# Windowed attention and two feed-forward layers on one core: blocks of 32 queries by 64 keys in place of 64 by 96, and an order of all steps read from a stored list

## The chip, the cores and the metric

The kernel runs on one core of a Trainium2 chip. The metric is the device time of one launch in microseconds (us), the median of several runs. Beside it there is one profiled execution, whose trace gives the start and end of every instruction and every transfer.

## What is computed

The reference, cut to what matters:

```python
def _attn_ref(q, k, v):                       # 4 x 8 x 576 x 64 (batch, heads, positions, width)
    scores = np.matmul(q, k.transpose(0, 1, 3, 2)) / np.sqrt(D)
    rel = pos[:, None] - pos[None, :]
    mask_plain = (rel >= 0) & (rel < 32)                        # heads 0 to 3
    mask_dil = (rel >= 0) & (rel < 128) & (rel % 4 == 0)        # heads 4 to 7
    scores = np.where(masks[None], scores, -1e9)
    attn = np.exp(scores - np.max(scores, axis=-1, keepdims=True))
    attn = attn / (np.sum(attn, axis=-1, keepdims=True) + 1e-09)
    return np.matmul(attn, v)

def _moe_ref(x, w_in, w_out, g_ln):           # 2304 x 512 -> 1024 -> 512
    h = x @ w_in
    sm = softmax(h)                           # max, exp, sum + 1e-9, over the 1024
    solu = h * sm
    ln = (solu - mean(solu)) / np.sqrt(var(solu) + 1e-06) * g_ln
    return ln @ w_out

def _moe2_ref(x, w_in, w_out):                # 2304 x 512 -> 2048 -> 512
    h = x @ w_in
    return (h * (1.0 / (1.0 + np.exp(-1.702 * h)))) @ w_out

def reference(...):
    x = _attn_ref(q, k, v) laid out as (batch * positions) x (heads * width)
    return _moe2_ref(_moe_ref(x, ...), ...)
```

A query looks at itself and 31 keys ahead of it; in the dilated heads these are every fourth position. If the positions of a dilated head are reordered into four streams, its window is 32 neighbours as well.

## The kernel before, in words

**Attention.** A batch has five *units*. Units 0 to 3 hold two heads each and the first 512 queries of both; the fifth, a half unit, holds the last 64 queries of all eight heads. That makes 16 full units and 4 half units. A full unit is cut into eight windows of `QW` = 64 queries by `KW` = 96 keys (the 64 and the 32 ahead of them). Its steps are small functions:

- `att_s` (TensorE): 16 score multiplications (line 235), one for each head and window, each with 64 rows (the width) by 64 queries as the weights and 96 keys as the moving columns. Two heads lie on two halves of the rows, two windows on two halves of the output partitions. In batches 0 and 1 (`PE_MASK`) two multiplications with an identity first put the mask into the result (line 231); in batches 2 and 3 VectorE adds it (`att_mask`).
- `att_max`, `att_sub`, `att_exp`, `att_sum` (line 301), `att_norm` (line 308) on VectorE, ScalarE and GpSimd: the softmax, over 768 columns of a full unit and 384 of a half one.
- `att_t` (TensorE): eight transposes of 128 x 96 (line 316), four into one bank of the PSUM, called once for each head; `att_p` copies each bank out (line 322).
- `att_x` (TensorE): 16 multiplications of the transposed probabilities with v (line 332): 96 rows, 64 columns of v as the weights, 64 queries moving. `att_y` copies the result into `x` (lines 350 to 358), in the order that the positions need.

`stir` (line 217) issues up to 16 filler multiplications ahead of some of these steps, as many as the planner's gap suggests.

**First feed-forward layer.** Weights arrive as raw 64-bit words, are converted to fp32 (lines 377 to 393) and split into a high and a low part (`split_hi`; `split_lo`, lines 441 and 445; `wo_l` is the low part of `w_out`). Each product takes three multiplications (high by high, low by high, high by low). Per tile of 128 tokens there are two halves of `h` (line 472, twelve records of 512 columns each), then the maximum (line 480), exp (486), the product with the softmax (494), the layer norm, transposes `lt` (523), and their split `lnh` (531) and `lnl` (534). For each 256 tokens the second product `y` follows (line 545). The first `y` needs the whole converted `w_out`.

**Second feed-forward layer.** Its weights are split while the first layer runs ("parked", lines 377 to 393 and 584 to 614) and written back to memory. The products are made in seven instead of eight block products (`h_prod` line 666, `o_plain` 748, `o_prod` 779), with sums on VectorE around them. At the end `ob` is summed (line 801) and stored.

**Order.** Every step is put into a `Plan` with a rank, an engine (or several), a cost, the steps it comes after, and slots that it takes and gives back (PSUM banks, buffers). `Plan.order` then plays the engines forward with these costs: whenever an engine is free, it takes the ready step of lowest rank. `emit` writes the steps in that order and ties each engine's instructions to it, so each queue is fixed before the launch. The ranks are worked out by the code from the lists `LOADS`, `HEAD`, `PARK` and others; the loads on SP's queue are steps too.

Of the kernel before, what the change touches and what calls it, by code (L numbers as in the profile page):

```python
# [24 lines left out]
QW = 64  # L25
KW = QW + 32
NW = S // QW
UB = 5
WM = NW - 1
# [32 lines left out]
class Plan:  # L62
# [5 lines left out]
    def add(self, rank, eng, cost, fn, after=(), take=(), give=(), lag=0.12, also=(), port=False):  # L68
        can = {eng: (cost, fn, port or eng == "POOL")}
        can.update({e: (c, f, port or e == "POOL") for e, c, f in also})  # L70
        self.works.append(Work(len(self.works), rank, can, after, take, give, lag))
        return self.works[-1]

    def order(self):
# [6 lines left out]
        while any(left.values()):  # L81
# [4 lines left out]
            for eng, works in left.items():  # L86
                while free[eng] <= t:
# [3 lines left out]
                    for w in works:  # L91
                        if any(t < r < t + w.can[eng][0] - 0.2 and w.key[0] - k >= 5 for k, r in soon):
# [41 lines left out]
def attention_moe_kernel(ctx, tc, qk, qk_last, v, v_last, masks, w_in, w_out, g_ln, w2_in, w2_out, out):  # L134
# [23 lines left out]
    for g in range(3):  # L158
# [20 lines left out]
    nq, nk, nv = WM * QW, WM * QW + 32, 2 * WM * D  # L179
    flat = [y1[g].rearrange("p k n -> p (k n)") for g in range(3)]  # L180
    lent = {2: (flat[0][:, 0:nq], flat[0][:, nq:nq + nk], flat[1][0:KW, 0:nv]),
            3: (flat[0][:, nq + nk:2 * nq + nk], flat[1][:, nv:nv + nk], flat[2][0:KW, 0:nv])}
# [14 lines left out]
    def load_v(idx):  # L197
        v_ = lent[idx][2] if idx in lent else ap.tile([KW, nv], F32, tag="v", bufs=VB, name=f"v{idx}")
        nc.sync.dma_start(v_, v[idx])
        vW[idx] = v_.rearrange("p (h w d) -> p h w d", h=2, w=WM)  # L200

    def load_last(b):

        t = ap.tile([P, 4, QW + KW], F32, tag="qkl", bufs=LB, name=f"qkl{b}")
        nc.sync.dma_start(t.rearrange("p i c -> p (i c)"), qk_last[b])
        vt = ap.tile([KW, 4, 2, D], F32, tag="vl", bufs=LB, name=f"vl{b}")
        nc.sync.dma_start(vt.rearrange("p i h d -> p (i h d)"), v_last[b])
# [14 lines left out]
    def att_s(n):  # L222
# [3 lines left out]
        if u < 4:  # L226
# [5 lines left out]
            for wp in range(4):  # L232
                for h, par in ((0, 0), (1, 1), (0, 1), (1, 0)):
                    rows, c = slice(64 * h, 64 * h + 64), QW * (2 * wp + par)
                    nc.tensor.matmul(ps[64 * par:64 * par + 64, h, wp * KW:wp * KW + KW], q_[rows, c:c + QW],  # L235
                                     k_[rows, c:c + KW], start=not masked, stop=not masked or wp == 3)
            sps[n] = ps[:, :, 0:4 * KW]
        else:
# [4 lines left out]
            for i in range(4):  # L243
                for h in range(2):
                    rows = slice(64 * h, 64 * h + 64)
                    nc.tensor.matmul(ps[rows, i * KW:i * KW + KW], last_w[b][0][rows, i, 0:QW],
                                     last_w[b][0][rows, i, QW:], start=not masked, stop=not masked or i == 3)
# [1146 lines left out]
```

## Time and profile before

| what | value |
|---|---|
| runs | 677.69, 676.4, 676.84 us; median 676.84 |
| span of the profiled execution (its time, first to last instruction) | 675.9 us |
| TensorE (PE) busy | 653.8 us, 97%, 4921 instructions |
| weight loads on TensorE (PEld) | 617.3 us, 91% |
| VectorE (DVE) | 524.2 us, 78% |
| ScalarE (ACT) | 386.6 us, 57% |
| GpSimd (POOL) | 126.3 us, 19% |
| DMA | 155.55 MB, mean 230 GB/s |

The span is 0.9 us under the median of the runs; no time of its own is given for the profiled execution beyond it. Busy time of an engine counts overlapping instructions once. PE's matmuls are pipelined: a row's duration is that of one instruction from start to end, while the next one starts before it has ended, so the cost of a stream is read from the distance of the starts. A group such as "x32" in the timeline gives the start of the first and the time to the end of the last. One `nc.tensor.matmul` with fp32 operands appears as two records (16 score multiplications are 32 records), one with fp32r or bf16 operands as one.

### The profile page before, as it was taken

The numbers are of one execution on the slowest core, as the hardware profiler recorded it, in microseconds if no ns is written. First come the engines' busy times: TensorE is split into PE (matmuls) and PEld (weight loads), VectorE is DVE, ScalarE is ACT, GpSimd is POOL, SyncE is SP. The second block draws the span as 40 slices with busy tenths as digits, with TensorE's granted clock in tenths as the row PEclk, the third lists the DMA queues.
The fourth block names the chain that finished last, engine by engine and source line by source line (L and its number), as shares of the span: only waits on it lengthen the run. The fifth ranks groups of instructions, "written<-read, shape, count | busy, mean of one in ns | idle before, by whom it ended". The sixth has DMA issues, their size and how long they took to land.

```text
span 675.9 us, 12935 instructions
## 1 busy us (share of the span) xinstructions
PE 653.8 (97%) x4921; PEld 617.3 (91%) x4921; DVE 524.2 (78%) x950; ACT 386.6 (57%) x789; POOL 126.3 (19%) x146
## 2 busy tenths in 40 slices
PE   6798999999999999999999999999999999999997
PEld 4676898888888898999999999999999999999997
DVE  3999977684776798789867899378699948778794
ACT  4898967485656776775335765242365534334552
POOL 0305373353532443433000000000000000000000
PEclk9889999999999999999999999999999999999999
DMA  8899126534221566986768886767699866679952
GB/s 294 287 309 284 49 88 238 186 134 153 73 100 63 197 243 228 324 304 216 270 225 290 310 292 241 280 242 285 232 312 329 297 227 206 238 247 319 328 184 84
DMA packets 58254, 155.55 MB, mean 230 GB/s; under 512 B 6608, under 2 KB 21968, under 8 KB 58192
## 3 DMA queue, kind: packets, MB, share of 16 engines
q1 hardware_dynamic: 58192, 154.72, 67.2%
q8 instruction: 39, 0.64, 0.4%
q14 instruction: 23, 0.19, 0.1%
HBM read 118.53 MB, written 36.18 MB: 229 GB/s over the span
## 4 chain that ended last, share of the span: by engine, by line
PE 74%; DVE 11%; DMA 8%; issue 2%; ACT 2%; POOL 1%; SPq 0%; ACTq 0%; DVEq 0%; POOLq 0%
PE hz L666 14%; PE h L472 12%; PE hx L666 11%; PE oz L779 10%; PE y L545 9%; PE ox L779 7%; PE ob L748 2%; PE ptp L316 2%; PE oa L748 2%; PE lt L523 2%; PE xt L332 1%; PE s L235 1%; DMA y<-in_w_in_dram 1%; DMA raw_('o', 3, 0)_4712<-in_w_out_dram 1%; DMA raw_('o', 1, 1)_3957<-in_w_out_dram 1%
## 5 line engine op out<-in xcount | busy, mean ns | idle before, releaser
L666 PE MATMUL hz<-yc,ws 128*128 128x384 f32 x576 | 107.5, 334 | 1.3 <-DVE u L678 1.3
L718 ACT CAST gs<-g 128x384 fp32r<-128x384 f32 x144 | 72.9, 514 | 59.1 <-PE oz L779 25.4
L666 PEld LDWEIGHTS hz<-yc,ws 128*128 128x128 f32 x576 | 100.5, 188 | 1.6 <-DVE u L678 1.6
L721 DVE TENSOR_TENSOR gs<-g,gs 128x384 fp32r<-128x384 f32 x144 | 78.2, 554 | 15.9 <-ACT gs L718 15.1
L666 PE MATMUL hx<-yc,ws 128*128 128x384 f32 x432 | 83.5, 335 | 2.0 <-DVE p L674 0.8
L545 PE MATMUL y<-lnh,wo_h 128*128 128x256 f32 x288 | 83.0, 288 | 0.0
L545 PE MATMUL y<-lnh,wo_l 128*128 128x256 f32 x288 | 81.5, 283 | 0.0
L545 PE MATMUL y<-lnl,wo_h 128*128 128x256 f32 x288 | 81.4, 283 | 0.0
L666 PEld LDWEIGHTS hx<-yc,ws 128*128 128x128 f32 x432 | 75.3, 188 | 3.2 <-DVE p L674 1.2
L472 PE MATMUL h<-wi_h,xh 128*128 128x512 f32 x144 | 58.9, 409 | 0.0
L472 PE MATMUL h<-wi_l,xh 128*128 128x512 f32 x144 | 56.4, 392 | 0.0
L472 PE MATMUL h<-wi_h,xl 128*128 128x512 f32 x144 | 56.4, 391 | 0.0
L545 PEld LDWEIGHTS y<-lnh,wo_h 128*128 128x128 f32 x288 | 55.1, 191 | 1.0
L545 PEld LDWEIGHTS y<-lnl,wo_h 128*128 128x128 f32 x288 | 55.1, 191 | 0.3
L545 PEld LDWEIGHTS y<-lnh,wo_l 128*128 128x128 f32 x288 | 55.1, 191 | 0.0
L695 ACT ACTIVATE sg<-g 128x768 f32<-128x768 f32 (+1 forms) x48 | 33.0, 687 | 32.4 <-DVE g L686 27.1
L695 ACT ACTIVATE sg<-hx 128x384 f32<-128x384 f32 x24 | 11.8, 492 | 50.8 <-PE hx L666 45.8
L779 PE MATMUL oz<-gs,wo 128*128 128x384 f32 x192 | 36.8, 335 | 0.0
L779 PE MATMUL ox<-gs,wo 128*128 128x384 f32 x192 | 36.7, 334 | 0.0
L308 POOL TENSOR_TENSOR t<-t,sx 128x768 f32<-128x768 f32 (+1 forms) x17 | 23.4, 1375 | 65.7 <-DVE sx L303 41.4
L779 PEld LDWEIGHTS oz<-gs,wo 128*128 128x128 f32 x192 | 33.5, 188 | 0.2 <-DVE gs L721 0.2
L779 PE MATMUL oz<-gs,w 128*128 128x384 f32 x192 | 33.6, 334 | 0.0
(391 smaller groups left out, 1412.6 us busy)
## 6 DMA issues: line engine op xcount, KB each, us to landing
ws<-wdq SPq DMA_DIRECT2D x48, 512.0 KB, 5.0
wo<-wdo SPq DMA_DIRECT2D x37, 512.0 KB, 5.3
ws<-wdq SPq DMA_DIRECT2D x48, 384.0 KB, 5.0
w<-wdo SPq DMA_DIRECT2D x48, 256.0 KB, 4.6
qk<-in_qk_dram SPq DMA_DIRECT2D x14, 528.0 KB, 5.2
v<-in_v_dram SPq DMA_DIRECT2D x14, 384.0 KB, 4.2
y<-in_w_in_dram SPq DMA_DIRECT2D x9, 512.0 KB, 4.9
wdq<-y SPq DMA_DIRECT2D x9, 512.0 KB, 3.0
```

The lines of the kernel that those rows point to most:

```text
L235: nc.tensor.matmul(ps[64 * par:64 * par + 64, h, wp * KW:wp * KW + KW], q_[rows, c:c + QW], k_[rows, c:c + KW], start=not masked, stop=not ...
L308: eng.tensor_tensor(t, t, wide(sms.pop(n), t.shape[1]), ALU.mult)
L316: nc.tensor.transpose(ps[:, j * P:j * P + P], t[:, 4 * h + j, :], ident)
L472: nc.tensor.matmul(hps[i][:, half, :], x[:, kt, :], w[:, kt, fs], start=(kt == 0 and j == 0), stop=(kt == KT - 1 and j == 2))
L523: nc.tensor.transpose(ps[:, j, :], es[i][:, f * P:f * P + P], ident)
L545: nc.tensor.matmul(yps[g, dm][:, 0:n], w[:, f, ds_], x[:, f, 0:n], start=(f == 0 and j == 0), stop=(f == NF1 - 1 and j == 2))
L666: nc.tensor.matmul(ps[:, 0:TB2], quad_weights(q, m, kk, a), yc2[m][:, x, kk, :], start=(m < 4 and kk == 0 and i == 0), stop=(kk == 1 and i ...
L695: nc.scalar.activation(sg, src, AF.Sigmoid, scale=1.702)
L718: nc.scalar.copy(gsp[jj, m][:, 0], o_block(jj, half, b))
L721: nc.vector.tensor_tensor(gsp[jj, m][:, 1], o_block(jj, half, b), f32(gsp[jj, m][:, 0]), ALU.subtract)
L748: nc.tensor.matmul(ps, w[:, (2 * k + a) * P:(2 * k + a + 1) * P], gsp[jj, 2 * half + b][:, x], start=first and i == 0, stop=last and i == 2)
L779: nc.tensor.matmul(ps, w, gsp[jj, m][:, x], start=m < 4 and first and i == 0, stop=last and i == 2, skip_group_check=True)
```

## The change

Blocks become `QB` = 32 queries by `KW` = 64 keys. A full unit has 16 blocks for each head. Its parts:

- **Scores.** 32 multiplications of 64 rows by 32 queries, 64 moving columns, on eight tiles of the array (two heads on the rows, four blocks on the output partitions), in a rotation written out. The mask multiplications have 256 columns for 384. A unit's softmax works on 512 columns for 768, a half unit's on 256 for 384.
- **Transposes.** Two neighbouring blocks of 64 keys are transposed together, 128 x 128, so a full unit has four transposes for eight, in one bank, and one copy of 128 x 512 for two of 96 x 512.
- **v** is laid out for 128 partitions: blocks of even and odd pairs on the two halves, each with its 64 keys, so a unit's v is 512 KB for 384. It is done on the host, as before.
- **Product with v.** 32 multiplications of 64 rows, 64 columns of v as the weights, 32 moving queries, into two banks; for the plain heads the output is written in runs of 8. `att_y` copies each bank by itself.
- **Order.** `add` takes the rank from the list `ORDER`, one number for each step, instead of the computed one; a few steps get one more predecessor, the costs of the attention steps are lower, a slot "mx" is new. The rule of `order` that lets a waiting urgent step hold back others no longer asks for a distance of five ranks.

```diff
-QW = 64
-KW = QW + 32
+QB = 32
+KW = 2 * QB
...
     def add(self, rank, eng, cost, fn, after=(), take=(), give=(), lag=0.12, also=(), port=False):
         can = {eng: (cost, fn, port or eng == "POOL")}
         can.update({e: (c, f, port or e == "POOL") for e, c, f in also})
+        rank = ORDER[len(self.works)] if ORDER else rank
...
-                        if any(t < r < t + w.can[eng][0] - 0.2 and w.key[0] - k >= 5 for k, r in soon):
+                        if any(t < r < t + w.can[eng][0] - 0.2 and w.key[0] > k for k, r in soon):
...
-        v_ = lent[idx][2] if idx in lent else ap.tile([KW, nv], F32, tag="v", bufs=VB, name=f"v{idx}")
+        v_ = lent[idx][2] if idx in lent else ap.tile([P, nv], F32, tag="v", bufs=VB, name=f"v{idx}")
...
-            for wp in range(4):
-                for h, par in ((0, 0), (1, 1), (0, 1), (1, 0)):
-                    rows, c = slice(64 * h, 64 * h + 64), QW * (2 * wp + par)
-                    nc.tensor.matmul(ps[64 * par:64 * par + 64, h, wp * KW:wp * KW + KW], q_[rows, c:c + QW],
-                                     k_[rows, c:c + KW], start=not masked, stop=not masked or wp == 3)
+            for m in range(4):
+                for h, j in ((0, 0), (1, 2), (0, 1), (1, 3), (0, 2), (1, 0), (0, 3), (1, 1)):
+                    rows, c = slice(64 * h, 64 * h + 64), QB * (4 * m + j)
+                    nc.tensor.matmul(ps[QB * j:QB * j + QB, h, m * KW:m * KW + KW], q_[rows, c:c + QB],
+                                     k_[rows, c:c + KW], start=not masked, stop=not masked or m == 3,
+                                     tile_position=(64 * h, QB * j))
...
-        for j in range(4):
-            nc.tensor.transpose(ps[:, j * P:j * P + P], t[:, 4 * h + j, :], ident)
-        ptps[n, h] = ps
+        for j in range(ns):
+            nc.tensor.transpose(ps[:, j * P:j * P + P], t[:, 2 * j:2 * j + 2, :].rearrange("p m k -> p (m k)"), ident)
+        ptps[n] = ps[:, 0:ns * P]
...
     def att_x(n):
+
         b, u = divmod(n, UB)
         pt = pts.pop(n)
-        ps = psB.tile([P, 512], F32, tag="B", name=f"xt{n}")
-        stir(ps)
-        if u < 4:
-            for w in range(8):
-                for h in range(2):
-                    nc.tensor.matmul(ps[64 * h:64 * h + 64, w * QW:w * QW + QW], vW[4 * b + u][:, h, w, :],
-                                     pt[:, h, w * QW:w * QW + QW], start=True, stop=True)
...
+        ps = [psB.tile([P, 512], F32, tag="B", name=f"xt{n}_{par}") for par in range(2)]
+        stir(ps[0])
+        plain = u < 4 and HPS[u] // 2 == 0
+        for c in range(2):
+            for j in range(4) if u < 4 else range(2):
+                for par, h in ((0, 0), (1, 1), (0, 1), (1, 0)):
+                    rows, out_ = slice(64 * par, 64 * par + 64), slice(64 * h, 64 * h + 64)
+                    if u < 4:
+                        w, x = vW[4 * b + u][rows, h, 4 * c + j, :], (2 * h + c) * P + QB * j
...
+                    if plain or (u == 4 and par == 0):
+                        o = o.rearrange("p (r j t) -> p r j t", r=4, t=8)[:, :, j, :]
+                        nc.tensor.matmul(o, w, pt[rows, x:x + QB].rearrange("p (r t) -> p r t", r=4), start=True,
+                                         stop=True, tile_position=(64 * par, 64 * h))
+                    else:
+                        nc.tensor.matmul(o[:, j * QB:j * QB + QB], w, pt[rows, x:x + QB], start=True, stop=True,
+                                         tile_position=(64 * par, 64 * h))
...
-        x = add(r, "PE", 1.2 * k, lambda n=n: att_x(n), ps_ + [done[vals]], take=("B",),
+        x = add(r, "PE", 1.1 * k, lambda n=n: att_x(n), [t, done[vals]], take=("B", "B"),
                 give=("pt", "v") if u < 4 and idx not in lent else ("pt",) if u < 4 else ("pt", "l"))
-        end[n] = add(r, "ACT", 0.6, lambda n=n: att_y(n), [x], give=("B",))
+        y = [add(r, "ACT", 0.4 * k, lambda n=n, p=p: att_y(n, p), [x], give=("B",)) for p in range(2)]
```

The stored list moves steps on every engine. In the rows below a name ends in a number that only tells buffers apart; `<-` separates what is written from what is read.

On TensorE, the transposes of a unit and what stands around them, before the change (`ptp` is the transposed probabilities, `s` scores, `mk` the mask, `lt` the layer norm's transposes, `xt` the product with v):

```order
L332 MATMUL xt_878<-pt_861,v_657 64x64 x16
L523 MATMUL lt_0_902<-ident,e_753 128x128 x4
L242 LDWEIGHTS ident_b
L242 MATMUL s_914<-mk,ident_b 128x384
L246 MATMUL s_914<-qkl_756 64x96 x8
L316 MATMUL ptp_0_927<-ident,t_796 96x128 x4
L316 MATMUL ptp_1_934<-ident,t_796 96x128 x4
L472 MATMUL h_948<-wi_h,xh_873 128x512
```

And the same steps of another unit, now:

```order
L319 MATMUL ptp_513<-ident,t_340 128x128 x4
L232 LDWEIGHTS ident_b
L232 MATMUL s_520<-mk,ident_b 128x256
L232 LDWEIGHTS ident_b
L232 MATMUL s_520<-mk,ident_b 128x256
L236 MATMUL s_520<-qk_412 32x64 x32
L218 LDWEIGHTS ident_b
L218 MATMUL xt_0_587<-ident_b 128x128
```

Two groups of four transposes have become one, and the score multiplications are twice as many with 32 queries and 64 keys each.

On TensorE, the start of the second product `y` of the first layer, before:

```order
L472 MATMUL h_1021<-wi_l,xh_895 128x512
L472 MATMUL h_1021<-wi_h,xl_939 128x512
L332 MATMUL xt_1096<-pt_1066,v_820 64x64 x16
L235 MATMUL s_1117<-qk_845 64x96 x16
L545 MATMUL y_0_1141<-lnh_900,wo_h 128x256
L545 MATMUL y_0_1141<-lnl_901,wo_h 128x256
```

And now:

```order
L492 MATMUL h_1406<-wi_h,xh_1360 128x512
L492 MATMUL h_1406<-wi_l,xh_1360 128x512
L492 MATMUL h_1406<-wi_h,xl_1364 128x512
L236 MATMUL s_1481<-qk_1064 32x64 x32
L565 MATMUL y_2_1522<-lnh_1323,wo_h 128x256
L565 MATMUL y_2_1522<-lnl_1324,wo_h 128x256
```

Ahead of the first `y` there stood eight halves of `h` (four tiles); now there stand ten (five tiles). In both a score unit is the last step ahead of it.

On VectorE, the last pieces of `wo_l`, for which the first `y` waits, before (`nm` is a maximum of `h`, `lnl` the low part of the layer norm, `sm` and `e` belong to the product with the softmax):

```order
L480 TENSOR_REDUCE nm_1040<-h_948 128x1
L534 TENSOR_TENSOR lnl_901<-lt_1_993,lnh_900 128x4x128
L445 SCALAR_TENSOR_TENSOR wo_l<-w1r_770,g_sb,wo_h 128x512 x2
L445 SCALAR_TENSOR_TENSOR wo_l<-w1r_684,g_sb,wo_h 128x512 x2
L491 TENSOR_TENSOR sm_1047<-sm_1047,eps_c 128x1
```

And now:

```order
L500 TENSOR_REDUCE nm_1387<-h_1262 128x1
L413 SCALAR_TENSOR_TENSOR w1r_1213<-w1r_1213 128x1024
L604 TENSOR_TENSOR y_1_80<-y_1_80 128x128
L554 TENSOR_TENSOR lnl_1324<-lt_1_1389,lnh_1323 128x4x128
L554 TENSOR_TENSOR lnl_1324<-lt_0_1398,lnh_1323 128x4x128
L511 TENSOR_TENSOR sm_1421<-sm_1421,eps_c 128x1
L512 RECIPROCAL sm_1421<-sm_1421 128x1
L514 SCALAR_TENSOR_TENSOR e_1420,mu_1439<-h_1262,sm_1421,e_1420 128x1024
L465 SCALAR_TENSOR_TENSOR wo_l<-w1r_1213,g_sb,wo_h 128x512 x2
L554 TENSOR_TENSOR lnl_1324<-lt_1_1430,lnh_1323 128x4x128
L500 TENSOR_REDUCE nm_1515<-h_1406 128x1
```

The last two `wo_l` now stand behind a product of `h` with the softmax and behind sums of parked weights (`y_1`, line 604), and one `lnl` stands between them and the first `y`.

## Rows read from the trace of the kernel before

**Rows 1.** The page's first line, and the busy time of each engine.

```profile
span 675.9 us, 12935 instructions
PE 653.8 (97%) x4921; PEld 617.3 (91%) x4921; DVE 524.2 (78%) x950; ACT 386.6 (57%) x789; POOL 126.3 (19%) x146
```

**Rows 2.** Windows: length, busy us of each engine, PE's granted clock, DMA share, GB/s.

```profile
0.00:78.15 78.15, 65.00 (x820) 52.59 (x821) 65.06 (x89) 61.21 (x123) 22.10 (x25) 0.93 0.81 259
...
82.00:310.00 228.00, 226.54 (x1996) 205.56 (x1985) 175.17 (x317) 155.10 (x345) 99.06 (x116) 1.00 0.54 183
82.40:671.80 589.40, 584.52 (x4032) 561.30 (x4028) 454.35 (x854) 321.20 (x659) 103.93 (x120) 1.00 0.67 229
```

**Rows 3.** Single multiplications of two lines: duration ns min/median/max, first and last start.

```profile
L235 PE MATMUL s<-qk x448: 242/243/419, 6.4 to 197.5; 64*64 64x96 f32 x150
...
L332 PE MATMUL xt<-pt,v x448: 222/222/316, 19.2 to 216.9; 96*64 96x64 f32 x150
```

**Rows 4.** Timeline around the first `y`: start us, us, engine, line, operation.

```profile
75.42 2.73 DVE L445 SCALAR_TENSOR_TENSOR wo_l<-w1r,g_sb,wo_h 128x512 fp32r<-128x512 f32 x4
...
81.54 0.89 PE L235 MATMUL s<-qk 64*64 64x96 f32 x32
...
82.36 0.39 PE L545 MATMUL y<-lnh,wo_h 128*128 128x256 f32 x1
```

**Rows 5.** Timeline of PE alone, 101 to 109 us.

```profile
101.81 0.28 PE L545 MATMUL y<-lnl,wo_h 128*128 128x256 f32 x1
101.93 0.28 PE L545 MATMUL y<-lnh,wo_l 128*128 128x256 f32 x1
...
102.50 1.15 PE L332 MATMUL xt<-pt,v 96*64 96x64 f32 x32
103.58 0.89 PE L235 MATMUL s<-qk 64*64 64x96 f32 x32
...
105.81 0.40 PE L472 MATMUL h<-wi_h,xl 128*128 128x512 f32 x1
...
107.88 0.39 PE L472 MATMUL h<-wi_h,xl 128*128 128x512 f32 x1
```

**Rows 6.** Timeline at 76 us: a unit's eight transposes and the next start.

```profile
76.29 1.04 PE L316 MATMUL ptp<-ident,t 128*96 128x128 f32 x8
...
77.16 0.60 PE L523 MATMUL lt<-ident,e 128*128 128x128 f32 x4
```

**Rows 7.** Timeline of the weight loads of one product with v, first two and four.

```profile
62.37 0.14 PEld L332 LDWEIGHTS xt<-pt,v 96*64 96x64 f32 x2 [0.36 <-ACT xh L455]
62.37 0.20 PEld L332 LDWEIGHTS xt<-pt,v 96*64 96x64 f32 x4 [0.36 <-ACT xh L455]
```

**Rows 8.** Groups of VectorE by line and shape: busy us, mean ns, idle before.

```profile
L301 DVE TENSOR_REDUCE sx<-t 128x8 f32<-128x768 f32 x16 | 15.1, 943 | 3.6 <-ACT t L286 2.3 <-ACT t L293 1.3
L301 DVE TENSOR_REDUCE sx<-t 128x4 f32<-128x384 f32 x4 | 2.2, 542 | 0.0
L308 DVE TENSOR_TENSOR t<-t,sx 128x768 f32<-128x768 f32 x2 | 1.9, 955 | 0.0
L322 DVE COPY pt<-ptp 96x512 f32<-96x512 f32 x10 | 6.7, 683 | 4.7 <-PE ptp L316 4.7
L480 DVE TENSOR_REDUCE nm<-h 128x1 f32<-128x1024 f32 x18 | 21.9, 1218 | 13.8 <-PE h L472 13.8
L494 DVE SCALAR_TENSOR_TENSOR e<-h,sm,e 128x1024 f32<-128x1024 f32 x18 | 23.1, 1284 | 0.7
L534 DVE TENSOR_TENSOR lnl<-lt,lnh 128x512 fp32r<-128x512 f32 x36 | 23.9, 681 | 3.6 <-ACT lnh L531 3.6
L389 DVE SCALAR_TENSOR_TENSOR y<-y 128x512 uint32<-128x512 uint32 x9 | 8.1, 905 | 4.0 <-ACT y L385 4.0
```

**Rows 9.** Waits of PE: us in total, times, longest us.

```profile
PE hz L666 <- DVE u L678: 1.3, 1, 1.3
```

**Rows 10.** Timeline: VectorE's last two sums, behind PE's last product.

```profile
671.33 1.08 DVE L801 TENSOR_TENSOR ob<-oz,op 128x384 f32<-128x384 f32 x2 [3.58 <-PE oz L779]
```

More of the change, by code (lines that the diff above doesn't have):

```diff
@@ L880, in attention_moe_kernel @@
-        ps_ = []
-        for h in range(nh):
-            t = add(r, "PE", 0.5, lambda n=n, h=h: att_t(n, h), [z], take=("B", "pt") if h == 0 else ("B",),
-                    give=("t",) if h == nh - 1 else ())
-            ps_.append(add(r, "ACT", 0.6, lambda n=n, h=h: att_p(n, h, nc.scalar.copy), [t], give=("B",),
-                           also=[("DVE", 0.7, lambda n=n, h=h: att_p(n, h, nc.vector.tensor_copy))]))
-        x = add(r, "PE", 1.2 * k, lambda n=n: att_x(n), ps_ + [done[vals]], take=("B",),
+            m = add(r, "DVE", 0.7 * k, lambda n=n: att_max(n), [s], take=("mx",))
@@ new lines, in attention_moe_kernel @@
+            m = add(r, "DVE", 0.7 * k, lambda n=n: att_sub(n), [m], take=("t",), give=free + ("mx",))
+            e = add(r, "ACT", 0.62 * k, lambda n=n: att_exp(n), [m])
+        else:
+            m = add(r, "DVE", 0.69 * k, lambda n=n: att_mask(n), [s], take=("t",), give=free)
+            m = add(r, "DVE", 0.68 * k, lambda n=n: att_max(n), [m])
+            e = add(r, "ACT", 2.7 * k, lambda n=n: att_exp(n), [m])
+        z = add(r, "DVE", 0.68 * k + 0.35, lambda n=n: att_sum(n), [e])
+        z = add(r, "POOL", 1.0 * k, lambda n=n: att_norm(n, nc.gpsimd), [z], port=True,
+                also=[("DVE", 0.68 * k, lambda n=n: att_norm(n, nc.vector))] if n in NORM_ANY else [])
@@ L890, in attention_moe_kernel @@
+        y[1].after.append(y[0])
+        end[n] = y[1]
     closed = add(-1, None, 0, end_attention, list(end.values()))
@@ L977, in attention_moe_kernel @@
                     del hl_end[u, part]
-                split_done[u, part] = w
+                split_done[u, part] = lo_ = w
                 if k < 3:
@@ L1120, in attention_moe_kernel @@
                         x.after.append(now[0, b])
+                    if b and half:
+                        x.after.extend(now[jj, k] for k in range(3))
             for d in range(2):
@@ L1160, in attention_moe_kernel @@
                     x.after.append(now[0, m])
+                if m == 3:
+                    x.after.extend(now[jj, k] for k in range(3))
             for d in range(2):
```

164 lines of the change are left out of this document (92 added, 72 removed), and 121 rows, old and new, of the table ORDER.

## The prediction

> **What bounds the kernel now.** I read the page's first line and busy shares, then the windows by stage, then the timeline of single units, and last the waits. TensorE (PE) is busy 97% of a span of 675.9 us [rows 1], so the first question is where it is not. The windows [rows 2] answer it. Up to 78.15 us PE shows 65.00 us, but part of that is filler (the `stir` multiplications of line 217), at a mean granted clock of 0.93; VectorE (DVE) shows 65.06 us in the same stretch. The first score multiplication starts at 6.4 us [rows 3], and the softmax on DVE needs scores, so after that DVE hardly rests, and PE is fed as fast as DVE converts weights and serves the softmax. From 82.4 us on PE is busy for all but a few us at full clock, while DVE, ScalarE and the DMA engines have room. So there are two regimes. Up to the first multiplication of the second layer (`y`, line 545, which needs all converted weights) the start is set by DVE; behind it every us of PE work is a us of time. The seam is visible [rows 4]: DVE's last weight split `wo_l` begins at 75.42 us and takes 2.73 us, PE's last score unit ahead of `y` starts at 81.54, and `y` at 82.36 us.
>
> **Scores.** A full unit is 16 small multiplications, which the chip runs as 32 records. In the timeline [rows 5] they take 0.89 us; the last one alone lasts 0.243 us (median of that line [rows 3]), so the starts spread over 0.65 us, 20.9 ns apart. Four tiles of 64x64 rotate, so one tile takes 4 x 20.9 = 84 ns for 96 columns. The product with v in the same rows: (1.15 - 0.222)/31 = 29.9 ns apart (0.222 is its median [rows 3]), two tiles, 60 ns for 64 columns. Both are about 0.9 ns per moving column, so the columns set the pace, and the pieces of different tiles run side by side. After the change a unit has 64 records of 64 columns on eight tiles, thus 8 rotations of 60 ns = 0.48 us where 8 rotations of 84 ns = 0.67 us stood: -0.19 us. Sixteen full units and four half units (whose eight rotations shorten alike, as their 32 records now sit on four tiles and not 16 on two) make 20 x -0.19 = **-3.8 us**. Eight tiles at once are nowhere in the trace. If only four run together, a unit has 16 rotations of 60 ns, +0.29 us and 20 times that +5.8; a gain beyond -3.8 would need less than 60 ns for 64 columns, and no row suggests one. I take the rotation, as both kinds of unit follow it.
>
> **Mask.** The 18 multiplications that put the mask into the scores of batches 0 and 1 shorten from 384 to 256 columns. 256 columns take 0.12 us in the `y` stream [rows 5], so 128 take 0.06: 18 x 0.06 = **-1.1 us**.
>
> **Transposes.** There were 144 and there are 72, each still 128 columns out. Eight take 77.16 - 76.29 = 0.87 us [rows 6], 0.109 each: 72 x 0.109 = **-7.9 us**. This is the largest term, and the surest, since the shape on PE is that of the layer-norm transposes beside it.
>
> **Product with v.** 16 multiplications of 64 columns over 96 rows become 32 of 32 columns over 64 rows, on four tiles. By moving columns a rotation would be 30 ns. But each piece still loads 64 columns of weights, and the load rows show what that costs: the first two loads of the unit run to 62.51 us, the next two, on the same two tiles, to 62.57 [rows 7], so a load takes some 0.06 us. It hides under 64 columns of movement and not under 32. So the rotation stays 60 ns, sixteen of them, as before: **0**. Bounds: 30 ns a rotation gives 16 x -0.030 = -0.48 us a unit, and 18 units' worth (four are half) -8.6 us; load and movement one after the other, 90 ns, give +8.6 us. I take 0, the row of the load being the nearest. The strided output of half of the units (runs of 8) has room under the same load: 32 columns may take twice as long.
>
> Sum on PE: -3.8 - 1.1 - 7.9 = **-12.8 us**. Of this, the part ahead of `y` lies in the DVE-set start and is worth something only if `y` starts earlier. So I ask what stands ahead of `y` in each order.
>
> **PE's order up to the first `y`.** The new order puts ten halves of the first layer (`h`) ahead of `y`, the old one eight. Two halves are 24 records, and nine of them pass from 105.81 to 107.88 [rows 5], 0.23 us each: +5.5 us. Nine full score units are there in both, and eight products; the cheaper ones save 9 x 0.19 + 1.0 + 32 transposes x 0.109 = 6.2 us; one half unit more adds 1.0. So PE has the same work ahead of `y` (+0.3 us), and nearly all of the 12.8 us, **13.1**, is missing behind it, where PE is the bound.
>
> **DVE's order up to the last weight split.** A pass over 768 columns takes 0.943 us, over 384 0.542 [rows 8]; 512 lie at 0.68. Twenty such passes (8 maxima, 8 sums, 4 subtractions) shrink: -5.3 us; one normalization of 0.955 [rows 8] fewer and one shorter, -1.2; one split of `x` fewer, about -0.8. More work is pulled forward: 3.5 copies of transposed probabilities (0.683 each, +2.4), one more `h` tile's maximum (1.218, +1.2), two more products of `h` with its softmax (2 x 1.284, and small ones, +3.2), one `lnl` more (0.681, +0.7), three passes over parked weights (0.905 each, +2.7) and small ones (+0.7), all from [rows 8]. Together +3.6: 65.1 + 3.6, with the same 13.1 us of rest, ends at 81.8 us; one `lnl` (0.68) still stands ahead of `y`, which then starts at about 83.0 where it started at 82.36: **+0.6 us**. Against it stand 128 KB more for each v transfer (384 KB before); the four of batch 0 are 0.5 MB, at the 259 GB/s of the window [rows 2] 2 us of transfer if the start waited for DMA. The new list issues the v loads later, behind the weights; I count 0 and keep +2 for the range.
>
> **Behind `y`.** From 82.4 us to PE's last product at 671.8 PE is idle for 589.40 - 584.52 = 4.9 us [rows 2], the longest wait 1.3 us, for a VectorE sum [rows 9]. The list reorders what stands around each of them. I can neither drop nor add one with reason, so they stay; all gone would be -5, twice as many +5. The end (two sums of 1.08 us and the last store after PE's last product [rows 10]) keeps its form.
>
> **Sum.** Span 675.9 + 0.6 - 13.1 = 663.4 us. The runs' median is 676.84, 0.9 above the span, so the runs should show **664.3 us**.
>
> **Rivals.**
> *The count of multiplications sets the pace (slower).* Mean spacing in a score unit is 20.9 ns, and no row shows a denser stream that lasts. If that is a floor per record, 64 records take 1.34 us: scores +0.67 us and products +0.41 (64 x 20.9 ns against 0.93), the half units' 32 records unchanged against 0.67. Sixteen times 1.08 = +17.3, with mask and transposes -9.0: +8.3 us behind an unchanged start, and **685 us**. It decides once the spacing stays above 13 ns in the scores and 15 ns in the product. For it: nothing in the trace goes below; against it: spacing follows the columns (20.9 for 96 on four tiles, 29.9 for 64 on two), which a floor would not do. 7%. The Trainium skill, "TensorE: Matmul & The Clock Gate", section "Wait - 56ns, not 53.3ns?", states that start-to-start never drops below about 25 ns however small the multiplication. By that rule 64 records would need 1.6 us a unit, scores and products together some 1.6 us more per full unit, and the time, an estimate by that page, would be near 693 us. This trace has 20.9 ns, under that floor, with four tiles in turn.
> *The order also closes waits, or the product runs at its columns (more gain).* The 5 us of waits go, or half of the -8.6: **659 us**. For it: the waits are few, and each is the end of a queue whose order is now another. Against: nothing shows which. 22%.
> *The start gets later, or new waits appear (less gain).* The saved PE time must be matched by DVE, which in the new order carries the fifth `h` tile before `y`; if its rests grow by 2 us, v's transfers cost 2 and one or two waits of 1 us come up: **669 us**. 14%.
> *The saving is not on the path (no change).* If behind 82 us another engine were the true pace, PE's smaller work would come back as rests: **677 us**. Windows speak against it: 175 of 228 us for DVE [rows 2]. 4%.
>
> **Numbers.** Forecast 53%, more gain 22%, less gain 14%, count as floor 7%, no change 4%. A measurement of this kernel can tell about 0.2%, 1.35 us, from no change. The forecast's own range, its unit costs being off by a quarter and the start by 2 us, is 660 to 669. The range that takes in most of both neighbours is 655 to 673. Faster by over 0.2%: 0.89; within: 0.03; slower: 0.08.
>
> **What would show it.** Score units of some 0.7 us in the timeline (0.89 before), transposes x72 at an unchanged distance of 0.109 us, products of v still near 1.1 us; the first `y` at 82 to 84 us; PE busy near 641 us; DVE's total down by some 15 us. Wrong would be: score units or products above 1.3 us (the floor), a first `y` beyond 86 us (the start), or the sum of PE's waits behind 85 us above 10 us (the order).

## The result, and the profile after

The change made the kernel slower: 683.62 us (median of four runs, 682.83 to 684.18) against 677.27 us for the kernel before on the same chip (four runs, 676.4 to 678.23). The ratio is 1.0082, with a 95% interval of 1.0059 to 1.0105. The forecast was 664.3 us. The profiled execution's span is 681.7 us, 5.8 more than before [rows 1].

The page's first line and busy times of the kernel after, and its row of granted clocks (40 slices of 17 us, in tenths):

```profile
span 681.7 us, 15060 instructions
PE 654.1 (96%) x6007; PEld 614.6 (90%) x6007; DVE 510.8 (75%) x942; ACT 374.5 (55%) x789; POOL 125.2 (18%) x154
PEclk9769999999999999989999999999999999999999
```

TensorE (PE) has 1086 records more, and its busy time has not fallen [rows 1], though the change was to shorten it by 12.8 us. VectorE's total fell by 13.4 us, near the 15 forecast. The windows of the kernel after (columns as in [rows 2]; the second begins at its first `y`):

```profile
0.00:78.15 78.15, 64.25 (x1370) 52.58 (x1371) 58.62 (x91) 53.48 (x116) 22.24 (x26) 0.87 0.76 277
90.30:677.60 587.30, 577.62 (x4466) 552.39 (x4460) 439.52 (x832) 311.09 (x652) 93.61 (x118) 1.00 0.68 228
```

Behind the first `y` PE now rests 587.30 - 577.62 = 9.7 us, where it rested 4.9 [rows 2], and PE's granted clock in the first 78 us is 0.87 where it was 0.93. The seam, from the timeline of the kernel after:

```profile
87.92 1.41 DVE L465 SCALAR_TENSOR_TENSOR wo_l<-w1r,g_sb,wo_h 128x512 fp32r<-128x512 f32 x2
...
89.51 0.86 PE L236 MATMUL s<-qk 64*32 64x64 f32 x64
...
90.30 0.39 PE L565 MATMUL y<-lnh,wo_h 128*128 128x256 f32 x1
```

The first `y` stands at 90.30 us, 7.9 later than before [rows 4]; the forecast was 0.6. From there to PE's last product it is 677.6 - 90.3 = 587.3 us, against 671.8 - 82.4 = 589.4 before: 2.1 gained, where 13.1 was forecast. So the forecast failed on both sides of the seam, and one of the signs that it had named, a first `y` beyond 86 us, came true. What PE does ahead of the first `y`, before and then after:

```profile
0.00:82.36 82.36, 69.21 (x893) 55.92 (x893) 69.20 (x96) 65.39 (x131) 22.29 (x26) 0.94 0.77 246
```

```profile
0.00:90.30 90.30, 76.40 (x1548) 62.19 (x1548) 70.63 (x110) 63.37 (x138) 31.60 (x37) 0.89 0.71 257
```

Its rests there are nearly the same, 82.36 - 69.21 = 13.2 us and 90.30 - 76.40 = 13.9; it is busy 7.2 us longer. PE's waits in the kernel after (us in total, times, longest):

```profile
PE hz L686 <- DVE u L698: 3.4, 11, 0.6
PE s L236 <- DMA y<-in_qk_dram: 2.9, 1, 2.9
PE s L232 <- DVE t L279: 2.7, 1, 2.7
PE hx L686 <- DMA ws<-wdq: 2.4, 1, 2.4
PE xt L349 <- issue: 2.0, 2, 1.3
PE h L492 <- DVE e L514: 1.8, 1, 1.8
...
PE s L236 <- issue: 1.2, 1, 1.2
```

Two things are new here. The wait for the sum `u` came once before [rows 9], now eleven times; and PE rests by "issue", that is with nothing in the profile to wait for, in the middle of units.

### The profile page after: what moved, and what is told of

The parts are those of the page before. It is cut to its first block, busy times and chain, and to the rows that moved or that the text cites. A ratio compares the mean times of both kernels' runs of the same rounds, so it can differ in the third digit from the quotient of the medians.

```text
span 681.7 us, 15060 instructions
## 1 busy us (share of the span) xinstructions
PE 654.1 (96%) x6007; PEld 614.6 (90%) x6007; DVE 510.8 (75%) x942; ACT 374.5 (55%) x789; POOL 125.2 (18%) x154
## 4 chain that ended last, share of the span: by engine, by line
PE 73%; DMA 10%; DVE 10%; ACT 3%; issue 2%; SPq 0%; DVEq 0%; ACTq 0%
PE hz L686 12%; PE hx L686 11%; PE h L492 10%; PE oz L799 9%; PE y L565 8%; PE ox L799 6%; PE oa L768 5%; PE ob L768 5%; DMA wo<-wdo 2%; PE s L236 2%; PE xt L349 2%; PE lt L543 1%; PE ptp L319 1%; DMA raw_('q', 6, 1)_3646<-in_w_in_dram 1%; DMA raw_('o', 6, 0)_3383<-in_w_out_dram 1%
## 5 line engine op out<-in xcount | busy, mean ns | idle before, releaser
L686 PE MATMUL hz<-yc,ws 128*128 128x384 f32 x576 | 112.7, 337 | 3.4 <-DVE u L698 3.4
L686 PE MATMUL hx<-yc,ws 128*128 128x384 f32 x432 | 86.2, 337 | 3.7 <-DMA ws<-wdq 2.4
L799 PEld LDWEIGHTS ox<-gs,wo 128*128 128x128 f32 x192 | 33.5, 188 | 0.4 <-DMA wo<-wdo 0.4
```

What stands on the lines that cost most here:

```text
L686: nc.tensor.matmul(ps[:, 0:TB2], quad_weights(q, m, kk, a), yc2[m][:, x, kk, :], start=(m < 4 and kk == 0 and i == 0), stop=(kk == 1 and i ...
L799: nc.tensor.matmul(ps, w, gsp[jj, m][:, x], start=m < 4 and first and i == 0, stop=last and i == 2, skip_group_check=True)
```

## Experiments

Each kernel was compared with the kernel before on its own chip. Three theories stood at the start: **A**, the blocks save what was forecast and the stored list loses it; **B**, the smaller blocks themselves hold PE up; and **K**, the lower clock of the start is the cause.

### 1 to 4: the list taken apart

```diff
-        rank = ORDER[len(self.works)] if ORDER else rank
```

> The changed kernel without its stored list: every step gets the computed rank, blocks and all else stay. Theory A (the blocks save PE time, and the stored list gives it back in waits and in a late start): behind the first y the waits fall back to those of the kernel before, the first y comes at 80 to 84 us (90.3 with the list), and the time is 664 to 668 us. Rival B (the smaller blocks themselves starve the start and bring the waits): first y still near 90 us, 680 us or more. Rival C (the list costs only part): 670 to 678 us.

Measured: 708.02 us, ratio 1.0446 (1.0404 to 1.0488), first `y` at 96.38 us. So the list is not worse than what the rules make of the new blocks; it is 24 us better. Theory A in this form fell. That the old rules were fitted to the old blocks is a guess; no run shows it.

For the next three, both orders were played through, and each step got the start that it has in one or the other:

```diff
+            at, eng = starts[1 if w.old < R2 - 1000 else 0][w.key[1]]     # 2: attention, first layer and input loads by computed ranks
...
+            at, eng = starts[1 if w.old >= R2 - 1000 else 0][w.key[1]]    # 3: the second layer by computed ranks
...
+            at, eng = starts[1 if w.sp and w.old < -90 else 0][w.key[1]]  # 4: the input loads by computed ranks
```

> Attention, first layer and all loads ahead of the second layer in the order of the computed ranks, the second layer in that of the stored list. Theory A: the start is repaired (first y at 80 to 84 us) and the many small waits of the second layer's products on VectorE's sums (3.4 us in 11 waits with the list, 1.3 us in one before) stay, so about 683 - 8 = 675 us. If the small waits come from the first part's order, it is like the run with all computed ranks. Rival B: no change, 680 us or more.

Measured: 718.23 us, ratio 1.0602 (1.0574 to 1.0630), first `y` at 96.34: no repair of the start, and 10 us more than with computed ranks throughout, with 5.6 us of waits for the sum `u` in 13 waits. The list's order of the second layer costs in this company too.

> The reverse: attention and first layer in the order of the stored list, the second layer by computed ranks. Theory A: first y stays at 90 us, the low clock from 25 to 46 us stays, the small waits of the second layer go: 683 - 6 to 10 = 673 to 677 us. Rival (the second layer's waits come from what the first layer leaves behind): no change, 682 to 685 us.

Measured: 674.97 us, ratio 0.9944 (0.9914 to 0.9973). With this alone the change is a gain, and some 8.6 us of the loss lie in the list's order of the second layer.

> The stored list for all but the 46 input loads of the first part, which stand on SP's queue where the computed ranks put them (the last load of w_out at place 29 and not 37). Theory L (the last load of w_out behind blocked loads of v makes the start late): first y at 83 to 85 us and 676 us. Rival P (PE's own queue, ten halves of h and a half clock up to 46 us, sets the first y, and PE has no gap ahead of it): first y within 2 us of 90 unless the clock changes too, 681 to 685 us.

Measured: 701.60 us, ratio 1.0389 (1.0324 to 1.0454), first `y` at 100.80, though the last load of `w_out` is issued eight places earlier. Theory L fell, and rival P's time with it. Why this order of loads costs 18 us is not shown: PE rests 18.4 us ahead of the first `y`, 8.5 of them by "issue" and only 2.1 in waits for a transfer.

A second look at the third kernel, for its profile:

> The kernel with only the second layer by computed ranks once more, for a profile (that of the first run holds a stall of almost 3 ms in its start and can't be read). Expected: 672 to 678 us, first y at 88 to 93 us as with the list, and PE's waits on the sums of line 698 at about 1.3 us in place of 3.4 us in 11 waits.

Measured: 670.47 us in the one run, first `y` at 88.06 us. No wait on that sum is left among PE's waits. From its first `y` to the end of the span this profile takes 668.7 - 88.1 = 580.6 us, where the kernel after takes 681.7 - 90.3 = 591.4 and the forecast had 663.4 - 83.0 = 580.4: behind the seam the blocks bring what was forecast, once the second layer has another order.

### 5: the blocks without any list

The cleanest separation gives the new blocks the order of before: every step on the engine and at the place that it has there.

```diff
+            at, e, gap, done = OLD[w.key[1]]      # of each step in the kernel before: start, engine, gap, end
+            w.start, w.eng, w.gap, w.done = at / 1000, E[e], gap / 1000, done / 1000
```

> The new blocks, every step on the engine and at the place that it has in the kernel before (both halves of a unit's transposes merged at the first of them); no rank is used. Theory A (the blocks are worth the PE terms that were predicted, and the order is what lost them): the first y at 79 to 83 us, as eight halves of h stand ahead of it, no small waits in the second layer, and some 5 us less between first y and the second layer: 667 to 671 us. Rival B (the doubled number of records stalls PE in the middle of units while the DMA engines are full, as the 3.2 us of such stalls with the stored list show): first y at 84 us or later and 672 to 680 us.

Measured: 673.87 us, ratio 0.9943 (0.9919 to 0.9968), first `y` at 83.05. The blocks alone are worth 4 us: the first `y` is at the edge of what A had, the time where B had it. PE's waits of this kernel:

```profile
PE s L198 <- issue: 4.3, 3, 2.6
PE hx L648 <- DVE yc L634: 2.6, 1, 2.6
...
PE ptp L180 <- issue: 1.8, 1, 1.8
...
PE xt L314 <- issue: 1.4, 1, 1.4
```

The "issue" rests are 7.5 us now, all but 0.4 of them ahead of 60 us. Where they lie says what they are. In the timeline of the kernel after, a product with v stops after 55 of its 64 records:

```profile
28.14 1.89 PE L218 MATMUL xt<-ident_b 128*128 128x128 bf16 x16
29.95 1.71 PE L349 MATMUL xt<-pt,v 64*64 64x32 f32 x55
32.99 0.44 PE L349 MATMUL xt<-pt,v 64*64 64x32 f32 x9 [1.32 <-issue]
```

Counting PE's records in the trace from its first, weight loads, multiplications and those of its sequencer alike, the longer ones of these rests begin in front of record 1217, 1986 and 2242 in the kernel after, 450, 705, 1218 and 1985 in the fifth experiment, and 450, 706, 1730 and 2497 in the first: each time 194 more than a multiple of 256, to one record. The pages list the transfers that bring instructions; the kernel before, then after:

```profile
q8 instruction: 39, 0.64, 0.4%
```

```profile
q8 instruction: 47, 0.77, 0.5%
```

Each is 16,384 bytes. PE's and PEld's records together, 9842 [rows 1] and 12014, divided by 256, are 38.4 and 46.9. In the kernel after three of these transfers land at 31.6, 48.8 and 55.2 us, and PE goes on at 33.0, 50.4 and 56.6. So PE had used up its instructions and waited for the next 256. The Trainium skill, "Runtime: NRT & Kernel Launch", section "Instruction fetch mechanics", states blocks of 16 KiB, 256 instructions, fetched while the current one runs, the cost mostly hidden. The block size agrees with these rows. That it is hidden does not hold for PE here: it rests 3.2 us in the kernel after, 7.5 in this one, and not once in the kernel before. What such rests cost in the end is asked further down.

### 6 and 7: the clock

```diff
-            stir(ps[:, 0, :])
+            stir(ps[:, 0, :], {2: 48}.get(n, 0))      # att_s: more filler ahead of unit 2's scores
-        stir(ps)
+        stir(ps, {5: 36}.get(n, 0))                   # att_t: ahead of unit 5's transposes
```

> The changed kernel with 48 more filler multiplications ahead of the third score unit of batch 0 and 36 ahead of the transposes in front of PE's 2.7 us rest at 23.8 us, so that PE does not rest for long between 15 and 26 us. Theory K (the rests brought the half clock from 25 to 46 us, and it cost some 8 us of the start): granted clock 1.0 up to 60 us, first y 4 to 8 us earlier, 676 to 680 us. Rival: the clock stays, or PE waits for data anyway and the saved time comes back as rests: 682 to 685 us.

Measured: 688.13 us, ratio 1.0149 (1.0122 to 1.0176), first `y` at 97.09. The half clock (a granted 0.5, thus 1.2 of 2.4 GHz) did not go. The profile's record of it has 23.9 us in the start, 20.5 in the kernel after and 10.2 in the kernel before; but that record begins only with a rise to full clock, at 11.3, 15.0 and 10.3 us, and the page counts what lies ahead of it as full. The rows do not: in the kernel after, the score unit at 13.43 us takes as long as the one at 27.02, which has a granted 0.50, and not as the one at 97.46, which has 1.00.

```profile
13.43 1.19 PE L236 MATMUL s<-qk 64*32 64x64 f32 x64
...
27.02 1.19 PE L236 MATMUL s<-qk 64*32 64x64 f32 x64
...
97.46 0.86 PE L236 MATMUL s<-qk 64*32 64x64 f32 x64
```

With that stretch, counted from the span's start, the half clock lasts 35.2 us here, 35.5 in the kernel after and 20.5 in the kernel before. The rest at 16.6 us shrank from 2.9 to 0.5 us, and PE waited later instead, in the middle of a unit and then for a bank:

```profile
PE xt L218 <- ACT xr L367: 4.4, 1, 4.4
...
PE xt L352 <- issue: 3.0, 1, 3.0
```

> Both: the second layer by computed ranks and the filler. If the two costs are apart (start and second layer), their gains add: 675 less 4 to 8, 667 to 671 us. If the filler gains nothing alone, 675 us.

Measured: 678.29 us, ratio 1.0008 (0.9987 to 1.0030): 3.3 slower than without the filler, as in the sixth experiment (4.5). Theory K's remedy fell: the filler left the half clock as long as it was, and its 168 records on PE cost more than the rests that they filled. What the half clock costs is not shown by it.

### 8: what sets the pace of the scores

```diff
                                      k_[rows, c:c + KW], start=not masked, stop=not masked or m == 3,
...
+                                         k_[rows, c:c + QB], start=False, stop=m == 3,      # 32 of 64 keys, batches 0 and 1
```

> The changed kernel, in which the score multiplications of batches 0 and 1 move only the first 32 of each block's 64 keys (half of the scores are left out). A score unit of 64 records takes 0.86 us with 64 columns, its starts 10.2 ns apart, where I had reckoned 7.5. Theory F (a floor per record): 10 ns apart again, 0.8 us or more. Theory C (columns, at a worse rate than with four tiles): about 5 ns apart, near 0.55 us.

Two score units of that kernel's timeline:

```profile
47.47 0.89 PE L239 MATMUL s<-qk 64*32 64x32 f32 x64
...
55.96 0.76 PE L239 MATMUL s<-qk 64*32 64x32 f32 x64
```

Their windows show different clocks (the value behind the brackets):

```profile
47.47:48.36 0.89, 0.89 (x69) 0.83 (x70) 0.24 (x1) 0.74 (x2) 0.35 (x1) 0.50 0.00 0
55.96:56.72 0.76, 0.76 (x66) 0.72 (x65) 0.00 (x0) 0.00 (x0) 0.00 (x0) 1.00 1.03 420
```

So the two rows can't stand for one pace. At full clock a unit takes 0.86 us with 64 columns (the seam above) and 0.76 with 32; with the last record's 0.216 and 0.192 us taken off, the starts come (0.86 - 0.216)/63 = 10.2 and (0.76 - 0.192)/63 = 9.0 ns apart in the mean. At half clock a unit takes 1.19 us with 64 columns (27.02, above) and 0.89 with 32. The mean hides two halves. In the unit at 97.46 us of the kernel after, the first 32 starts are 7.7 ns apart and the last 32 are 12.1; with 32 columns, in the unit at 55.96, it is 5.2 and 10.4. Units of 32 records, in the tenth experiment below, stay at (0.46 - 0.216)/31 = 7.9 to the end:

```profile
49.63 0.46 PE L200 MATMUL s<-qk 64*32 64x64 f32 x32
```

So the columns count in a unit's first half, and from the 33rd record on it is mostly the count of records. Theory F's 0.8 us or more and theory C's 0.55 both missed; F's floor describes the second half alone. Why the 33rd record is the border is not shown. The time was 683.49 us in one run, against 683.62 for the kernel after.

### 10 and 11: fewer records

```diff
+            for _ in range(3 if masked else 0):
+                nc.tensor.matmul(ps[:, 0, 0:4 * KW], ident_b, mk[:, HPS[u] // 2, :], start=True, stop=True)
...
-            for m in range(4):
+            for m in range(2 if masked else 4):
```

> The new blocks in the order of before (673.87 us, stalls of 7.5 us in PE's own stream up to 60 us, each at a multiple of 256 PE instructions behind a 16 KB instruction transfer), with half of the score records of the full units of batches 0 and 1 left out (512 instructions fewer on PE) and three filler multiplications of 256 columns in their place, which take about the time that was taken away (0.36 against 0.33 to 0.4 us a unit). Theory I (PE runs dry of instructions in the dense units): the stalls fall to 4 us or less, the first y comes 2 to 4 us earlier, 669 to 672 us. Rival (the rests come from elsewhere and only look so): stalls and time unchanged, 673 to 675 us.

Measured: 670.85 us, ratio 0.9897 (0.9871 to 0.9923); first `y` at 79.14, 3.9 earlier than in the fifth experiment. PE's waits hold no "issue" row any more:

```profile
PE ptp L283 <- POOL t L275: 2.9, 3, 1.2
PE s L200 <- DMA y<-in_qk_dram: 2.6, 1, 2.6
PE hx L650 <- DVE yc L636: 2.5, 1, 2.5
PE xt L313 <- DMA v<-in_v_dram: 2.5, 1, 2.5
```

So theory I holds for the rests: with fewer records they are gone. It does not show what they cost. The stretches ahead of the first `y`, in the fifth kernel and in this one:

```profile
0.00:83.05 83.05, 68.71 (x1452) 56.55 (x1452) 61.89 (x95) 59.88 (x130) 20.30 (x26) 0.86 0.74 261
```

```profile
0.00:79.14 79.14, 64.03 (x1219) 51.92 (x1219) 61.75 (x95) 59.76 (x130) 20.22 (x26) 0.89 0.76 273
```

PE rests 15.1 us here and 14.3 there: the rests by "issue" have become waits for data. The whole 3.9 us are PE's busy time, which fell by 4.7. About 1 us of that is that the filler took less time than the scores left out. The half clock is shorter too, 25.0 us for 38.0 (counted as in the sixth experiment), and the run can't tell how much of the gain is due to that.

```diff
-            nc.tensor.matmul(bank[:, 0:P], ident_b, ident_b, start=True, stop=True)
...
+        for _ in range((n + 1) // 2):
+            nc.tensor.matmul(bank[:, 0:4 * KW], ident_b, mk[:, 0, :], start=True, stop=True)
```

> The new blocks in the order of before, with each two filler multiplications of 128 columns (four instructions) made one of 256 (two instructions): same PE time, some 90 instructions fewer ahead of the first y. Theory I: the boundaries move, and the stalls fall by about 90 parts in 2000, hardly to be seen in the time: 672 to 675 us. If the filler's own form matters for the clock, the half clock (24 us in this order) changes by 3 us or more and the time by 1.5.

Measured: 673.63 us, ratio 0.9943 (0.9923 to 0.9963), first `y` at 82.16. The rests by "issue" fell from 7.5 to 3.4 us, more than expected, and the time did not follow:

```profile
PE s L203 <- issue: 3.4, 2, 2.7
```

The recorded half clock fell from 23.9 to 10.2 us, but here the record begins only at 27.8 us. The wide filler shows what lies ahead of it, seven multiplications of 256 columns in the first row and eight in the second:

```profile
25.42 1.70 PE L185 MATMUL s<-mk,ident_b 128*128 128x256 bf16 x7
...
28.88 1.04 PE L185 MATMUL s<-mk,ident_b 128*128 128x256 bf16 x8
```

Their starts are 213 ns apart in the first and 109 in the second, so PE ran at half clock up to there, and in sum for 38.0 us in this kernel and 38.0 in the fifth. The filler's form did not change the clock, and what the half clock costs in the order of before stays open.

### 12: the eleven waits

The seven block products of a pair (`h_prod`, line 686) are chained: the sum `u` (line 698) reads the bank of the third, and the sixth adds into the same bank. In the kernel before PE takes them in their own order, with the fourth and fifth between. The list lets only one product stand there. The timeline of the kernel after shows what that does:

```profile
565.82 1.21 PE L686 MATMUL hz<-yc,ws 128*128 128x384 f32 x6
566.09 0.56 DVE L694 TENSOR_TENSOR p<-hx,p 128x384 f32<-128x384 f32 x1 [1.59 <-PE hx L686]
566.56 0.55 DVE L724 TENSOR_TENSOR g<-g,sg 128x384 f32<-128x384 f32 x1
567.03 0.55 DVE L698 TENSOR_TENSOR u<-hz,p 128x384 f32<-128x384 f32 x1
...
567.63 1.15 PE L686 MATMUL hz<-yc,ws 128*128 128x384 f32 x5 [0.61 <-DVE u L698]
```

One product takes six starts of 0.17 us, about 1.04; `p`, one other pass and `u` take 1.5, and PE waits 0.61.

```diff
+        for ms in self.rows:               # the seven products of one pair
+            for w, at in zip(ms, sorted(w.key[0] for w in ms)):
+                w.key = (at, w.key[1])
```

> The changed kernel with one thing of its list undone: of the seven block products of each pair in the second layer (line 686) the list lets the sixth, which writes again into the bank that the sum of line 698 reads, follow with only one product between; here PE takes the seven in their own order at the places that the list gives to them, with two products between, as in the kernel before. Nothing else of the list moves. Theory D (this distance is what makes PE wait for the sums: 11 waits, 3.4 us, and as much again in starts that come late without a gap): these waits go, 683.6 - 5 to 8 = 676 to 679 us. Rival V (VectorE's own order puts other work ahead of the sums and is the cause): the waits stay, 682 to 685 us.

Measured: 675.49 us, ratio 0.9972 (0.9953 to 0.9991). One edit of the list gives 8.1 us back (7.5 by the two ratios). The profile puts it behind the first `y`, which stands at 89.87, almost where it was:

```profile
89.87:673.40 583.53, 574.65 (x4465) 551.34 (x4460) 440.29 (x833) 310.24 (x651) 93.49 (x118) 1.00 0.69 231
```

From there to the end it is 583.5 us for 591.4, 7.9 less. PE rests 4.9 us less behind the seam, 2.9 of them in the waits for `u`, and is busy 574.7 us for 577.7: the starts that came late without a gap. Of the waits, one is left:

```profile
PE hz L706 <- DVE u L718: 0.5, 1, 0.5
```

Theory D holds for the waits. Rival V is not shut out in full: VectorE's steps of the second layer are played through anew once PE's move, and some changed places. Two or more other passes stand between `p` and `u` in three of the 24 chains now, and in seven in the kernel after. How much of the 8.1 us came by that was not tested.

## Why the prediction was wrong

The forecast was 664.3 us; 683.6 came out, 19.3 more. By the runs, that is 8.1 us for the order of the seven products (the twelfth experiment), 675.5 - 673.9 = 1.6 for the rest of the list against the order of before (the intervals of those two overlap), and 673.9 - 664.3 = 9.6 that the blocks fall short by without any list. By the profiles the span is 18.3 us over the forecast: the first `y` came 7.3 late, and from there to the end it took 591.4 us for 580.4, 11.0 more. My rival of less gain had both, a later start and new waits, at some 5 us together and 14%.

**Behind `y`: the step that failed most.** "I can neither drop nor add one with reason, so they stay." There was a reason to be had. The order of PE showed the seven products of each pair in their own order before and in another one now; the names of the banks tell which product writes what a sum has just read. I had compared the two orders only up to the first `y`, where attention lies, since the change is called one of attention. The bound that I gave, twice as many waits for +5 us, held for the rests (9.7 us for 4.9) and was too small for the whole: PE's products also started late without a gap, and the twelfth run puts all of it at 8.1 us. A wait of some tenths costs little once; here it came eleven times, in a chain that repeats 24 times.

**Scores: the size was wrong.** The rotation of eight tiles was to give -0.19 us a unit. It runs at 10.2 ns a record in the mean where 7.5 were reckoned: the first 32 records of a unit keep near the rotation, 7.7, and the last 32 do not, 12.1 (the eighth experiment). What failed is to take the pace of one rotation for that of 64 records in a row. From one step's start to the next a unit takes 98.24 - 97.46 = 0.78 us now, 104.40 - 103.58 = 0.82 before [rows 5], so it gives 0.04, and 20 times that is 0.8 us of the 3.8. The timeline of the kernel after:

```profile
97.46 0.86 PE L236 MATMUL s<-qk 64*32 64x64 f32 x64
98.24 0.38 PE L565 MATMUL y<-lnh,wo_h 128*128 128x256 f32 x1
```

My rival of a floor was right that the count comes in, and wrong in its price: 20.9 ns is no floor, as the starts come 7.7 to 12.1 ns apart, and it costs 3 us against the forecast, not 21. The Trainium skill's 25 ns ("TensorE: Matmul & The Clock Gate", section "Wait - 56ns, not 53.3ns?") does not hold for eight tiles in turn, with 7.7 and 12.1 measured; the measurement decides.

**The start: "PE has the same work ahead of `y`", and VectorE sets it.** With the list the first `y` was forecast at 83.0 and came at 90.3. PE has no rest from 56.6 us on to 90.3, so PE's own queue and not VectorE's set it. That could have been read before: in the kernel before VectorE's last `wo_l` ends at 75.42 + 2.73 = 78.15 us [rows 4], `y` starts 4.2 us behind it, and PE has no wait from 58 us on to `y`. So the term that failed is +0.3 us for PE's work ahead of `y`: its rests grew by 0.75 and its busy time by 7.2. The start-to-start distances of PE's records ahead of `y`, without rests and summed by step in the two traces, say where that lies. The two more halves of `h` cost 5.8 us (5.5 reckoned), and transposes and mask save 4.6; but, with half a unit more in each, the scores save nothing and the products with v take 3.5 us more, and the filler takes 2.2 more. What changed under all of them is the clock: 35.5 us of half clock for 20.5. I had priced every step from rows at full clock. The kernels after, of the ninth and of the twelfth experiment have the same order up to the first `y`; it stands at 90.30, 88.06 and 89.87 us with 35.5, 25.2 and 32.6 us of half clock. At that rate, 2.2 us for 10.3, the 15.0 us more than before would be some 3.2 us of the delay, an estimate from these three profiles. The rests by "issue" (3.2 us) are no further loss in the sum of rests, which hardly grew. In the order of before VectorE is busy 57.06 us of the first 78.15, against 65.06 before [rows 2], and `y` still did not come earlier than 83.05.

**Transposes, mask, product with v: right at full clock.** Six transposes pass in 101.87 - 101.22 = 0.65 us in the kernel after, 0.108 each as before, and there are 72:

```profile
101.22 0.82 PE L319 MATMUL ptp<-ident,t 128*128 128x128 f32 x6
101.87 0.60 PE L543 MATMUL lt<-ident,e 128*128 128x128 f32 x4
```

A product with v goes from 76.50 to 77.56 us where the next step starts, 1.06 against 1.08 before [rows 5]; the forecast was 0. That holds at full clock; ahead of `y`, where much of it runs at half clock, it took more, as said.

**What stays open.** Of the 9.6 us by which the blocks fall short, 3.0 are the scores' second halves. In the fifth profile PE's products with v, the same halves of `h` and the filler ahead of `y` take 4.5 us longer than in the kernel before (distances of starts, as above), with 38.0 us of half clock for 20.5; and PE rests 2.9 us more, 1.2 ahead of `y` and 1.7 behind it. These 10.4 us cover the shortfall but are measured side by side, not tested one by one. The wait of 2.6 us on `yc` at the start of the second layer (0.5 before) is one of the rests; in the eleventh experiment it is 0.9, with the time as it was. Whether the rests by "issue" bring the longer half clock, and what each of them costs, is open: in the tenth experiment both shrank together, in the eleventh the rests alone, and there hardly anything was gained.

Four versions beat both kernels (experiments 3, 5, 11 and 12); the fastest are the new blocks in the order of before, with the plain or the wide filler, 673.9 and 673.6 us, 0.6% under the kernel before.

## What to carry to other kernels

When a change comes with a new order of everything, compare the orders to the end of the program and not only where the change is named: look for chains in which a product writes again to a bank that another engine has yet to read, and count what stands between. Price small multiplications by their count as well as by their columns, and a start in which PE rests at the clock that it has there, not at that of the steady part. Where the record of the clock begins late, read the clock from the pace of a known row. And test a new order and a new tiling apart: here one was worth 4 us and the other cost 10.

## What the runs showed of the hardware

At full clock, starts of multiplications on 64x32 tiles, eight in turn, come 7.7 ns apart for the first 32 records of a unit and 12.1 for the last 32 with 64 columns, 5.2 and 10.4 with 32 columns; at half clock the unit takes 1.19 and 0.89 us in place of 0.86 and 0.76. PE takes its instructions in blocks of 256 records, each a transfer of 16 KB; where 64-record units stand close together it stops at the block's border, up to 3.5 us at a time, while the page names "issue"; with 512 records fewer those stops were gone. The record of the granted clock begins 8 to 28 us into the profiles that were compared here, and the pace of PE's rows ahead of it is that of half clock. And more filler in the start, put in to keep PE from resting, left the half clock at 35 us and made the kernel 3.3 to 4.5 us slower.
